# Another stored order, other PSUM banks and other eviction engines for a two-headed layer on one core

## The chip, the cores and the metric

The kernel runs on one core of a Trainium2 chip. The metric is the device time of one execution in microseconds. Three executions of the kernel before took 272.57, 272.51 and 273.82 us, a median of 272.57. The engines are named as the profile names them: PE (TensorE matmul), PEld (its weight load), DVE (VectorE), ACT (ScalarE), POOL (GpSimd) and SP (SyncE), whose queue issues nearly all DMAs.

## The reference

Two independent layers on 2048 tokens of width 640, concatenated along the features.

```python
# A: short filter, gate, long convolution by FFT, gate
k_shift = sum(k_pad[:, t:t+S] * shift_k[:, ks-1-t] for t in range(4))
kv = k_shift * v
y = irfft(rfft(kv, 2*S) * rfft(ssm_k, 2*S))[:S] + kv * ssm_D
a = q * y
# B: 32 heads of 20, four segments of 512 tokens, a memory carried from segment to segment
q, k, v = x @ wq, x @ wk, x @ wv
for s in range(4):
    p = softmax(q_s @ k_s.T * scale + causal_mask)
    a_mem = (phi(q_s) @ M) / (phi(q_s) @ z + 1e-6)     # phi(t) = t + 1 or exp(t)
    o = sigmoid(beta) * a_mem + (1 - sigmoid(beta)) * (p @ v_s)
    M, z = M + phi(k_s).T @ v_s, z + phi(k_s).sum()
b = o @ wo
out = concat(a, b)
```

## The kernel before

The program is recorded first and issued afterwards. `conv`, `project`, `attend` and `project_out` call proxies that store every operation (line 150, `Recorder.add`) with its dependencies; matmuls that belong together make one operation, and operations that share PSUM make a group. `issue` (line 247) then issues all 1543 operations in the order that the packed table ORDER gives, and binds each of the 486 PSUM groups to the bank that the packed table BASE gives. PSUM is one tile, `ps`, of eight banks of 128 x 512 f32. All instructions carry line 256, the line of the issuing call, so the rows are told apart by their tiles. The semaphore waits follow from the dependencies and the banks, so the order on each engine and the bank numbers decide who waits for whom: an engine takes its instructions in order, and an instruction that waits holds up all behind it.

Layer A (`conv`, line 428) goes over five slices `dp` of 128 features. The filter `ssm_k` is brought to `kT` with time on the partitions, by PE transposes for slice 0 and through a DRAM copy (`turned`) for the others. `k` arrives transposed in `kr`; the short filter is PE work against diagonal matrices `skd` (`ks` groups), and DVE multiplies by `vt`. `spectrum` (line 515) makes DFTs with the table `Wf`, whose results are evicted to `F` (`FK` for the filter, `FX` for the signal), with butterflies on DVE into `Kh` and `Xh`. `product` (line 548) is DVE alone (`pq`, `Y`), and `inverse` (line 584) is PE against `Wi` and a DVE multiplication by `q` in `pq`.

Layer B goes over eight units u: segment s = u // 2 and a half of the heads. `project` (line 636) computes K, Q and V from `xT` against `wqkv`, five matmuls of 320 columns for each 128 tokens, evicted to `KQ` and `Va`. K and Q are transposed to `KQT` (by PE for u = 0, by DMA otherwise), `phi` goes to `PP` and `PqT`. A bound on the scores is worked out from the largest |k| (`kmx`, transposed on PE, reduced by DVE into `kam`, then `A`, `qabs` and `bT`) and four small DMAs write it as a row of `KQT`. `attend` (line 722) makes scores on PE in row groups of 32, 384 or 256 columns wide below the diagonal, and with a mask from `pack` on the diagonal. ACT turns each two banks into `ET` by an exponential of 1024 columns, 160 of them in all. PE then sums values (`Va` with `ET`) and memory (`Mbd` with `PqT`), and DVE divides (`rr`, `o`, `o_s`). `project_out` (line 815) multiplies by `wo`; for the last segment PE transposes `o_s` into `xT` first, and the outputs are evicted to `PP` and `outb`.

An eviction copies a PSUM group to SBUF. `evict` (line 387) looks up which engine does it in the string EVICT (line 863), a digit for each of 238 evictions: "1" is DVE, "0" ACT.

```python
    def evict(self, out, in_, grp):
        e = self.evicts
        self.evicts += 1
        if EVICT[e] == "1":
            self.nc.vector.tensor_copy(out=out, in_=in_, grp=grp)
        else:
            self.nc.scalar.copy(out=out, in_=in_, grp=grp)
```

Twenty warm-up matmuls on a cleared tile `o` stand at the start of PE's order. They write nothing that is used.

Of the kernel before, what the change touches and what calls it, by code (L numbers as in the profile page):

```python
# [865 lines left out]
ORDER = r"""
c-jTQ1ArU=3<SVzHo3ZA+qP}nwr$&A+qP}nwr$(iOpwHu2ohIHNIZ!z2_&H;lEjikl1eg3E-56Xh@=uqYDpt$C7q;~@KRn>%1Q>wBjqH&l$LN(QZh;fsV!wBl0Zx{NlnQsrKGw<m3&fF>PTd9sU}6Gve
b}PQbjUL0VyOArLF{|zEqTY(o$kdEh#7sB%W51XwqDYNfgN{4JC!f*W%Jb3QH2rqbW6?7LiPvSMzITZ7hu>fo9QS+C-X4NJ*-xG=yZ;_R?00Yct6v9VL#mmeg88OKL7nsG+2Tl+t#RMRIE=DXm|%jbza
1l1!89S}CGsw7(S9vN}Kp${@+8ou#MrmU7xfx=MHHE4`$=c9T9*K?`XC%`VxrpY)K5nnTiPPARBqHCPJk3>_k?q_U3J2^vF&%4*4>Id!J4lflwhr)hRgr@3XARMolKM4M`Qt)z)`xFpu~vP4J7G94+?b
&V|5c{)l)OI@9>%e9`a(FIyxCu%KSCZT1FRMBd>Nw&x&t*v#mx;E3XvRXID9BrY|xLLMJE?K3Eb-Xm!jS`)+bhaLnaWYjK=vrMa6C{X@w4olB1CosEGy;=zpG=a2l8_UnhdNfuWZ5AtH4($edTphxwWs  # L870
cq_BvI1X?(7b4LU`(Ne7M1Hri1)>L%SSvn2s{%68c=d*q0;)lNE4kID+&D}!{V1nU-EshxGQZq|01f?Kt#PSI&HLuN^6Y|}2<U867@=SdCirYYG^r%P1!*JH9sE=UN(VE_yDgdCT}a#FS{5E9`zK(EOn
oi97Jw_cP}(pOK*ZjH+uGDkw8riQ^_9jWQqM{mg`Ny|MtSFXzr9i^i+1Jm=SMCLBNEJO5;+?CrhM$gDlP0C?<PBQX}oR`x&Tw}=s8LK1otc=rGyeelkEHd$gp3zf!Ptq_I!{MYZl>3sJS@=*6X*`C<5s
ie%2*P2#tM@blmdH>pm8^Uq_w}e=(TEtv$8t;+k7PQt@v08wa30sEvR|LbAok}Bj$n2k(1V(Tw=@@X@|uoeG+fuc`b^I0dA*}Ca9c0vMct=2^tnXGO^t=HlA8mV05Or7v5|)_<$*TB1ip}&Oo)1TsQEa
N1$apx=_JnLWJcsG$xGsyCT1c;;$@A&7y3q?>uX8Ew-U^l9LvObC-3F4KGl~R1+VmpzSgKH$kH6gH(H4A)$mn5=t6$f`7FbDD9g|CNvAMA;^2dPl)@as{2a;8`bDO4Fyo>zX7iK0)lvMSO;CdKSc*R+3
DV)6CdE&wk2y?^1<Zhw{3AvASCU~gGvWgmF+Ga$n`A;tq(K%eW^txPMShp2$cz@K%t}mwZ1^QhnH9~E3)7ebMYxICQI5Hh6Xp3^LfU5LK^0bIH7?^8R%a+{%?hl|Hmt$?sKdHk&be&MnyklW2yJ0(1>3
PcYq337vMn00HCk{y+hG+GS_iIX8?@pQwnR(j!y4vAD+F00Ys84Qmj9$N3!n+xBbGH~B#UjSkQyD3*a|`r!QxndM6-r$#^zkl!sv`1?1G-`#klrOd$S`uVgOQDAMQgZcIG-BL3B%ET^QLqp)dZb@VlnA
e)y+_(3MdPjA7lljoX>hx-*si(!TtmX)J*iL0a3vpBmM6au<JVJPT{_Z3C5uSQN=^H~(mQ>xv^BZ4EHV(%E5lgLASKM=|tcI2&kt7~V?Y0LEAb>y6M1a4-8{KT08^mBv1nM0XtJF>YkA9p?$2WLXTd9y
rCy7;Ir!2KzbI4sx6wU@z;5-j>xaGm~v)X6uEDxXLU>_OXyGhbydvn>6;dLx^c-c$N)O9_JW}r+J>)>;iA`Hj`QfWVee<X7~AkdF&b=av<{B6dQ#byu(~J)oNf6uJbMj;~+-ZBi>_8JmwQV<t65{U_9e
^8-ka7#o_jvIV`um;WP}zXpF#f&an`jXaj7d&9q4vhiZ7ik$B6)n2yQFXS3`b``IoOu-R4}?>QdRY&iPcbQ@+vte_3UTpNQzHo=Y}zs;~>_S)vzF$}f&HUU*I7A0&V3fmM^MR8kTMXadRLP?v7@>anXS
}CiIiZ%n4thAM}%C^WB+i6s>vbMw;+Zh~3Ih&2>-qh-%i8ZiB7Q?IB3DiM6pM_C&5;GCj8(Ms?Ys)MwtJz0Zw{Tw1>RSz)i``giH7%;2!g8x+(Y&@L_Gae3!UF!4aeNM1SQ~3=pV-{yA)>Fb`Jmr~`EA  # L880
@nBwv7b7TK?2rF~<2i|ZY%rQJbjPvW7xj;*q!ehq7_wRN<MSZ52-%EEYZzl2|0jNja1oox}i*fzV2PS({{TQ`f~TkSJ9T6as~J?sj;aI+=yA57r8>?b!_Z2!)lw%fXU4<F$PeUDv7OpoGA(9ZW@r2k<`
--~6qfmps2+bxwZ#||6hJFSDK_FzxrXR+5h`g)}G^Eik0zRxaT1y*9e9k7Fz&JWpPJ7Ryi8tMI_{o_%)WNXmZFWXuS@PSS{ZpZ9|owO^q3Yoo+ueW4wcFNqs`&Bz_{rrpt?5v5wuGu*Y^09sw7c8US$1
uN#O*n7YZ5<xqh7I?Z*o=p`X-{$29^szdw+#Lq&+q~d>@^<RIDdsV$nKA<t7r1}81Fg#mUZ(F_>3)>=sElg?$~X6Y+I4b-y)As@{f38Pw)xv@YHhqGkb22k;TV&Hh*CSyo*ovmzLEFc?kcCDIU@{;0LC
9LC@>ouo2s^9liZK@_R)u?D@QiSMpa@)Q5U8-vPDCKHaBzb+6&SP~2<!PR#HPR>FJwPgL<zKGS=7C$H+Ay`)$3(q6{PdI<Z2H&)JT`D`!m4Sbf*@!H<d8+l#-jS61J8+(6$YxVuJy|X4>&%fATEcXxA)
c@hVt@MvJ!58`ppX;JuZLlx)dA`W!`zM2bvjslNRhxNpZ{aPyl`nDX5FhP7Y^k?))1S7=+qmmrTjt;GpRM(_zRuVCY7gid-|b;_gNM^!w$V5F9uJ}7d;PZ^^v%A-L+MukWAMX%$hY}+-{E0&ryutle$u
1qP2cCCHKd;K{T@s2cyx`e2RxD<@m+q`Px)y->SsK%p7rp0(Qo-VKjxP_j-Ge*sCvOK`xU?KL3+<MaNqy>RgbIBJfeQ_Yku7y_(PANU;T&wa|V9;FaPZpkia+hz$1U}&;7AK@faFKU-)<b;4$@&Bk<7!
f!F@jU-~D1<FEX!zw^)jAN3y$Z2
"""
# [76 lines left out]
```

## Time and profile before

| | |
|---|---|
| median of three runs | 272.57 us |
| span of the profiled execution, first to last instruction | 272.0 us |
| PE busy | 260.8 us, 4368 matmuls |
| DVE busy | 250.9 us, 424 instructions |
| ACT busy | 248.8 us, 388 instructions, 160.6 us of it in the 160 exponentials |
| DMA | 43.74 MB, mean 161 GB/s |
| mean granted clock of TensorE | 0.993 |

The busy time of PE counts a matmul from its start to a modelled end, and matmuls overlap, so 96% does not mean that PE could take no more. In a timeline row the first number is the start, the second the time that the row covers, then come engine, line, operation, tiles and shapes, and in brackets the idle time of the engine before it, with what ended it. In a row of windows the busy time of each engine stands with its count of instructions, then the granted clock as a share of full speed, the DMA share and GB/s. The profiled execution has no separate time of its own in the table: its span is 0.57 us below the median.

### The profile page before, as it was taken

Reading aid. Unit: us, or ns where it says so; the run is one execution under the profiler, and the core shown is the slowest. Engines: PE = TensorE matmul, PEld = TensorE weight load, DVE = VectorE, ACT = ScalarE, POOL = GpSimd, SP = SyncE. Lnnn points to the kernel's source line nnn. Section 1 sums busy time; section 2 is a strip of 40 time slices with the busy share of each in tenths; the row PEclk is TensorE's granted clock in tenths of the full one; section 3 lists DMA queues with packets and bytes.
Section 4 is the critical chain, followed back from the end, with each engine's and each line's share of the span. In section 5 each row is a group of like instructions: output and inputs, shape, how many; then the busy total and the mean of one; then the engine's idle time right before and its main releaser. Section 6 shows DMA issues by size and latency. Waiting matters only on the chain.

```text
span 272.0 us, 10130 instructions
## 1 busy us (share of the span) xinstructions
PE 260.8 (96%) x4368; PEld 195.4 (72%) x4371; DVE 250.9 (92%) x424; ACT 248.8 (91%) x388; POOL 6.9 (3%) x18
## 2 busy tenths in 40 slices
...
PEclk9999999999999999999999999999999997999999
...
GB/s 166 347 207 243 82 191 225 311 194 172 170 217 201 144 195 195 191 178 159 159 165 190 116 151 226 147 197 65 146 177 82 4 154 27 169 155 90 27 68 133
DMA packets 126972, 43.74 MB, mean 161 GB/s; under 512 B 117339, under 2 KB 124512, under 8 KB 126800
## 3 DMA queue, kind: packets, MB, share of 16 engines
...
q8 instruction: 34, 0.56, 0.9%
q0 software_dynamic: 160, 0.20, 0.2%
...
## 4 chain that ended last, share of the span: by engine, by line
PE 55%; ACT 33%; issue 6%; DVE 4%; ACTq 0%; DVEq 0%
PE ps L256 55%; ACT ET L256 21%; ACT F L256 4%; ACT KQ L256 3%; ACT PP L256 3%; ACT outb L256 1%; ACT Va L256 1%; DVE F L256 1%; DVE pq L256 1%; DVE Kh L256 1%; ACT bT L256 1%; DVE qabs L256 0%; DVE vt L256 0%; DVE Xh L256 0%; DVE PP L256 0%
## 5 line engine op out<-in xcount | busy, mean ns | idle before, releaser
L256 ACT ACTIVATE ET<-ps 128x1024 bf16<-128x1024 f32 x160 | 160.6, 1102 | 1.9 <-PE ps L256 1.7
L256 PE MATMUL ps<-wqkv,xT 128*128 128x320 bf16 x480 | 76.3, 300 | 0.5 <-ACT ET L256 0.3
L256 PEld LDWEIGHTS <-xT 128*128 128x128 bf16 x640 | 58.1, 98 | 25.7 <-issue 5.2
L256 PE MATMUL ps<-Va,ET 128*128 128x21 bf16 x1280 | 42.4, 172 | 0.3 <-ACT ET L256 0.3
L256 ACT CAST F<-ps 128x512 bf16<-128x512 f32 x69 | 42.0, 687 | 0.3 <-PE ps L256 0.3
L256 PEld LDWEIGHTS <-ET 128*128 128x128 bf16 x1280 | 39.7, 96 | 3.0 <-issue 2.2
L256 PE MATMUL ps<-KQT 32*128 32x128 bf16 (+2 forms) x896 | 34.6, 240 | 1.1 <-ACT ET L256 1.0
L256 PEld LDWEIGHTS <-Wf 128*128 128x128 bf16 x320 | 28.9, 97 | 6.1 <-issue 1.5
L256 ACT CAST KQ<-ps 128x320 bf16<-128x320 f32 x61 | 28.2, 496 | 1.4 <-PE ps L256 1.3
L256 PE MATMUL ps<-wo,xT 128*128 128x320 bf16 x160 | 25.4, 299 | 0.0
L256 PEld LDWEIGHTS <-KQT 32*128 32x128 bf16 x896 | 16.0, 92 | 10.9 <-issue 9.9
L256 PE MATMUL ps<-vt,Wf 128*128 128x256 bf16 x160 | 22.4, 272 | 0.1
L256 PE MATMUL ps<-kT,Wf 128*128 128x256 bf16 x160 | 22.2, 273 | 0.2 <-ACT ET L256 0.2
L256 PE MATMUL ps<-Y,Wi 128*128 128x256 bf16 x160 | 21.7, 280 | 0.0
L256 DVE TENSOR_TENSOR o<-ps,rr 128x640 bf16<-128x640 f32 x24 | 19.5, 814 | 0.2
L256 PE MATMUL ps<-Mbd,PqT 128*128 128x84 bf16 x96 | 18.1, 202 | 1.2 <-ACT ET L256 0.9
L256 DVE TENSOR_TENSOR Y<-Y,pq 128x2048 bf16<-128x2048 bf16 (+1 forms) x20 | 18.6, 945 | 0.0
L256 DVE TENSOR_TENSOR pq<-Xh,Kh 128x2048 bf16<-128x2048 bf16 x15 | 18.1, 1209 | 0.0
L256 PEld LDWEIGHTS <-Wi 128*128 128x128 bf16 x160 | 15.3, 100 | 3.5 <-issue 1.0
L256 ACT ACTIVATE PP<-KQ 128x640 bf16<-128x640 bf16 (+1 forms) x18 | 17.7, 991 | 0.0
L256 PE MATMUL ps<-pack 32*128 32x128 bf16 x512 | 14.7, 216 | 1.9 <-ACT ET L256 1.7
L256 ACT CAST Va<-ps 128x320 bf16<-128x320 f32 x31 | 15.0, 520 | 1.2 <-PE ps L256 1.2
...
## 6 DMA issues: line engine op xcount, KB each, us to landing
...
```

What stands on the lines that cost most here:

```text
L256: f(*[fix(a) for a in args], **{k: fix(v) for k, v in kw.items()})
```

## The change

The program, its operations and their shapes stay. Three tables are replaced: EVICT, ORDER and BASE. In EVICT 36 of 238 digits differ, and DVE has 29 evictions instead of 31, ACT two more. ORDER is another order of the same 1543 operations, which differs on every engine and in SP's queue, and BASE gives other banks. The rows of the two packed tables say nothing to a reader and are cut to their first line.

```diff
-EVICT = ("10000010100101001001010000000000000000000000000000000100000000000000010100000000000000111000000000100000000000000000000000001000000000000000"
-         "00000000000000000001001110000000000000100000000001001010010000000000010000000001000000000110000101")
+EVICT = ("1101000001000110000100110000000000000000000000000000000000000000000000010000000000000011100000000000100001000000000000000000000000000000"
+         "000000000000000000100010000100000001000000010000001001010000010010000000010000000001010001000000000000")
 ORDER = r"""
-c-jTQ1ArU=3<SVzHo3ZA+qP}nwr$&A+qP}nwr$(iOpwHu2ohIHNIZ!z2_&H;lEjikl1eg3E-56Xh@=uqYDpt$C7q;~@KRn>%1Q>wBjqH&l$LN(QZh;fsV!wBl0Zx{NlnQsrKGw<m3&fF>PTd9sU}6Gve
...
+c-jrt(_$D35CqWK+1=E(ncB8(+qP}nO4`)6ZQHhO8~6Uhc{ov!011%@iID_xkrY5OltLWjLvjQn1yUjvQX>sYqdf8>BC;SW3LpkzqBu&RB#5*~hxCYmvdDmpD1!<pf{Mt5Y^a3n$bq8B422;oav~Q5<xm|pQ46&Z
...
 BASE = r"""
-c-mD{0TRO?2m=KC|Br_uST|2?tAvoS5RoNW!|TcG*+eC3oHwmElk>~^V))`X+nCC;UDJSLb*jKgL@M4F(9Vs<SL{6w-p0wfWta-o#YiQusNKmznMv_Q$k*|7#;ND9Qp7iYl3QQ~ZgdS+yJPJ*!Jgb3rz
...
+c-lo%3l_sL2-0Zu{x_Zi>DHIdzd~%ASy<YgQ|5Dy^;lM3kB#QzT~Ex@^WX3sc=nx$PuMqaW42z7yxPTaRStL$&c^T^k~g;$TT|~v_BU6I9+>u^+RkX`w^@{ZH0G}Dz|QIUE5xv-p(@ciX5E}Z)<uuj1b1Q&e1`so
...
```

Four places of the new order, in words. At the start, two tiles of x are loaded before the first part of the DFT table, and the transposes of `kT` and x stand between warm-up matmuls on PE. In the segment s = 3, half 0, a value projection and the `kmx` transposes stand before a group of masked scores that they followed. In the segment s = 1 the `kmx` transposes stand behind masked scores that they preceded. At the end, all eight last output evictions are on ACT.

More of the change, by code (lines that the diff above doesn't have):

```diff
@@ L865 @@
 KQW, FW, WW = 1, 1, 1
 ORDER = r"""
-c-jTQ1ArU=3<SVzHo3ZA+qP}nwr$&A+qP}nwr$(iOpwHu2ohIHNIZ!z2_&H;lEjikl1eg3E-56Xh@=uqYDpt$C7q;~@KRn>%1Q>wBjqH&l$LN(QZh;fsV!wBl0Zx{NlnQsrKGw<m3&fF>PTd9sU}6Gve
-b}PQbjUL0VyOArLF{|zEqTY(o$kdEh#7sB%W51XwqDYNfgN{4JC!f*W%Jb3QH2rqbW6?7LiPvSMzITZ7hu>fo9QS+C-X4NJ*-xG=yZ;_R?00Yct6v9VL#mmeg88OKL7nsG+2Tl+t#RMRIE=DXm|%jbza
-1l1!89S}CGsw7(S9vN}Kp${@+8ou#MrmU7xfx=MHHE4`$=c9T9*K?`XC%`VxrpY)K5nnTiPPARBqHCPJk3>_k?q_U3J2^vF&%4*4>Id!J4lflwhr)hRgr@3XARMolKM4M`Qt)z)`xFpu~vP4J7G94+?b
-&V|5c{)l)OI@9>%e9`a(FIyxCu%KSCZT1FRMBd>Nw&x&t*v#mx;E3XvRXID9BrY|xLLMJE?K3Eb-Xm!jS`)+bhaLnaWYjK=vrMa6C{X@w4olB1CosEGy;=zpG=a2l8_UnhdNfuWZ5AtH4($edTphxwWs
@@ L871 @@
[L871 to L886, printed above, removed]
@@ L887 @@
-f!F@jU-~D1<FEX!zw^)jAN3y$Z2
+c-jrt(_$D35CqWK+1=E(ncB8(+qP}nO4`)6ZQHhO8~6Uhc{ov!011%@iID_xkrY5OltLWjLvjQn1yUjvQX>sYqdf8>BC;SW3LpkzqBu&RB#5*~hxCYmvdDmpD1!<pf{Mt5Y^a3n$bq8B422;oav~Q5<xm|pQ46&Z
+4Q)^#1yL8p;HZNJh=)9=iW-Q7$f%5JXoz|UKqFK^Av8vG6h=$5LO$ka6J%jlreZTBWNPMO0VZNo6l6)3U@0bM5~g7>wnht-W=Eu8XOv-Creu2*XD4()2jpg3v_mY!MmB~<T4rK7W@mY3W^;5!H*`l23`8F0Wnc70
+AM{603`Q9ALj|ryC=9|7ROA3uVr3@hTxMV|EaOlN$2=C{a?WQUGcpHraskuvE2}a+gE$PqY|7@G$yuDjsSJyxY{p3}%E?^9rL4{>tj}a@$U<C&btudcXuvwG%Nop$dfbFj7>W4Ei`5*Bu^5L97=!UxjrEv-nry+A
@@ new lines @@
++=69j#Wf6JOr6b1*oZZlh&ha<TTzXhv6hq3i0jyxO&CeH;Q;nwJN9EL_Fz3%@E~?z3RZG2W^gfAu_HS%vWCM>q|k7ZQfFfqc4IjX;V^1(1ADO#d$TjAVI#M26F0Lp+c2JX;S988JGSRmZsTAMVOJ*6>FB^z+KoY&
+g`_%^sWliOn8uk%q|=#LyR#?b>k&lP+B}M5*vTGT$OO8Gix5KxFoL=a<UA}!L><Jw?8lQ>iQPPbG0dRHv4?XojAOY1r!ky!(Vtf^f+Kkf>GcwBVH7j!Ud~4*&8*`%o)dT#S@br}AV4PaGP3Cn+{6W3#5IiOS?pja
+xsKC3%QHNO^9Umgun^fbq29q=+`|c;WN3*f+j)qQ<P@XnVaC=t8ddHxtlY;DK14Kmfbg;eOA$dHA&uVWQQl)@8LY>+kH?uqqexuc#UUC+uP~~L1nOg4Wm?_OgKQ<&c%3=*0G}eACX_@nN=Iuhy}?_2g7|WWH~9=x
+HGxdi+)Bx#w|S1|d4U&siB04IpW`wga)c(+y!sN4m{pVONR2J|w1B?A1bv0L5>Li!9GR%k_?#+}HL<+p8%)ur@`|tdhHsff^6Lw}#y}mU!8%iu%3~&zcPy+=*-V~rmd2E~h$ZhCq6>A5eqdRhujTb4-=Um-;#hr;
@@ new lines @@
+&n%)JFk9znbcrFQw6vN`*BSbSW%Mh)p}3aNkNAv|`U%P93;tlJ4%5F#AwLi(KQT`$YZc8TnWd<vlkcdi3v`_R!dy)+)ii_rMoOu!i!_T&(u`6=vq}XmriFC4R?^h+L2GI*X(_d|qNb8Ol2;b%CatZTHAt6gHpwl^
+G>0^owi?>%Xm+WqTQsNSllEFr>uG&$pzSoQg|mj*LY8ZIgt122K|AUSZ7;2~pmfre+FCnETUn*6wSYvjHk!oNXgf)2-?>&JTN7=nQLMG(myVJ~zA>sb)8^Vz3rh=aBmdAz3Q00cZtFC@C9t>_)3)hf?$9L~%ZkcB
+Zr9G*MZ0P@{l(b!gYm4frm~;xrM<O}{wAcmc9$MfM0#jy>n{VOr>3#Kn%4U1PTi$3ES>e&Vv^pXS#;a239Y!Km6UcwGTM4Qq(>CGRZEDdYXb>yL+uX(bg&)Pk`lp&*&a<~LoAbxv%Nai_Q^i&Do6F0PP4=|-bzU~
+39Hm_T1NKk0X?oKw6vVmKpUW^bf9d|gPPeoOA0$6WhJx@k}eWPPwRfUtXDLPWwqX-+Q<4xc_}9m?W$(CzBa)&>P@XIre}1b-PW^uPS5KFZ78?2r}UD(a$oz&L(OJY<f7)VoR+~FNkzG&(`|-TkV?|e`rBZ6pw~2?
@@ new lines @@
+-O&72ORno39V(6Go{p7AT2&tF6Md?8b%>0UiBemh=>QuhFZGo^*WvO)U+WvqWs{_kz14R*%LZBvsVVO@$O>C-D`KOigiW$IHp+%uNgE^6WwecuQg%?rScr|6sWL%=ZH`U0K~_yh*eIE8)1;^sv$<AXf~1bjv&k|;
+f@OgnmAX>gN?UlHA{DKYm9ffJ#SY0rD{IGOrcAMNR^ARvRa<0>t(sM^(~{TnSW|0eOYF5BmopN}o7-$@WR0!5oscG$(3jdtnI*A3hR?J_eo8{*qmHy?Hc|>$D2?g$t%23BnpVqdTODg?bEK|?_Xxh+T39`qD=X})
+e$!pj%G~SAJXvWi?Yi8M03T}?WxlkwOVZW~+JgV-m|vA^64vKiJ!@lI?6dBct+r6wS$q4U9jv2uvbDC(!ud^EW$}EQMe$#{(QZj+i|Ud6w{Eidp1?O-7mMbfw5uiaMbgc>TXOGVJuQyM^~G{tF34rMBE9Uk+>xZd
+%l6n0{i!{@mxuAavfDcNSve<(J&A9(ofhazB&F}LWs=I5%U@0HOJ%in@-&{-S4d~?Z4v#u{?l~6M@D;e|D%z-qmS|QzSs8K5FhIMEQKGigLcRcTLxb#{rrga_lvg1GI~~5TPK<Qk{z`{e%X%OdRZl_<%F3H_LDZj
```

11 lines of the change are left out of this document (8 added, 3 removed).

## The prediction

> **What bounds the kernel now.** I read the page first, for its sums and its clock row.
>
> ```profile
> span 272.0 us, 10130 instructions
> PE 260.8 (96%) x4368; PEld 195.4 (72%) x4371; DVE 250.9 (92%) x424; ACT 248.8 (91%) x388; POOL 6.9 (3%) x18
> PEclk9999999999999999999999999999999997999999
> ```
>
> Three engines are nearly full, so no average tells which one matters. One slice in 40 shows a TensorE clock below full. The chain of waits, in order of time, comes next; its first and last long pieces are these (start, us, engine).
>
> ```profile
> 1.26 18.64 PE ps L256 x147
> 19.95 12.40 PE ps L256 x116
> 32.41 8.88 PE ps L256 x116
> ...
> 254.90 13.70 PE ps L256 x220
> 268.62 0.43 ACT PP L256
> ```
>
> The start belongs to PE without a hole, and so does the end. Between them the chain hops between ACT's ET (the exponentials) and PE. So I cut the span at the first and the last exponential on ACT, whose timeline rows are these, with every wait of ACT over 0.2 us that lies between them.
>
> ```profile
> 33.66 1.98 ACT L256 ACTIVATE ET<-ps 128x1024 bf16<-128x1024 f32 x2
> 116.47 0.43 ACT L256 CAST KQ<-ps 128x320 bf16<-128x320 f32 x1 [0.25 <-PE ps L256]
> 117.25 3.77 ACT L256 ACTIVATE ET<-ps 128x1024 bf16<-128x1024 f32 x4 [0.35 <-PE ps L256]
> 227.45 5.61 ACT L256 ACTIVATE ET<-ps 128x1024 bf16<-128x1024 f32 x6 [1.34 <-PE ps L256]
> 259.30 2.03 ACT L256 ACTIVATE ET<-ps 128x1024 bf16<-128x1024 f32 x2
> ```
>
> The table of windows for the three parts (length; then busy us of PE, PEld, DVE, ACT, POOL; granted clock; DMA):
>
> ```profile
> 0.00:33.66 33.66, 32.29 (x279) 23.88 (x282) 23.35 (x42) 20.20 (x42) 6.94 (x18) 1.00 0.85 210
> 33.66:261.33 227.67, 221.29 (x4002) 166.31 (x4002) 222.64 (x374) 225.47 (x341) 0.00 (x0) 0.99 0.83 156
> 261.33:272.00 10.67, 7.25 (x94) 5.26 (x90) 4.87 (x10) 3.11 (x7) 0.00 (x0) 0.99 0.35 103
> ```
>
> The middle is ACT's: busy 225.47 of 227.67 us, 2.20 idle, of which the three waits are 0.25 + 0.35 + 1.34 = 1.94. DVE idles 5.03 there. The whole is 33.66 + 227.67 + 10.67 = 272.00. The median of the runs, 272.57, is 0.57 above this span; I carry the 0.57 along. A difference under 0.5% (1.36 us: 271.21 to 273.93) cannot be told from none.
>
> **The change part by part.** No instruction is added or dropped except that 36 evictions change engine, so each term is a matter of when.
>
> *Work on ACT in the middle.* Counted from the digits of EVICT and the stored order, ACT has 95 casts of 320 columns and 68 of 512 between its first and last exponential before, 93 and 69 after. The price of one in a run of them comes from two rows.
>
> ```profile
> 25.14 2.68 ACT L256 CAST F<-ps 128x512 bf16<-128x512 f32 x5
> 36.29 1.48 ACT L256 CAST KQ<-ps 128x320 bf16<-128x320 f32 x4
> ```
>
> A cast alone takes 0.59 and 0.43 there, so the next ones cost (2.68 - 0.59)/4 = 0.52 and (1.48 - 0.43)/3 = 0.35. The term is -2 x 0.35 + 0.52 = **-0.18 us**. DVE, with 5.03 of slack, covers the one 320-column cast more (13 for 12) that it gets, against one 512-column cast fewer (5 for 6).
>
> *The stretch at half clock.* ACT's wait of 1.34 us has a cause. The table of windows in steps of 3.4 us, at the two emptiest windows for PE and the two after:
>
> ```profile
> 81.60:85.00 3.40, 2.59 (x40) 1.81 (x41) 3.40 (x6) 3.40 (x5) 0.00 (x0) 1.00 1.24 225
> 221.00:224.40 3.40, 2.33 (x61) 1.63 (x58) 3.37 (x7) 3.40 (x5) 0.00 (x0) 0.94 0.98 173
> 224.40:227.80 3.40, 3.40 (x27) 2.02 (x25) 2.76 (x4) 2.06 (x4) 0.00 (x0) 0.56 0.06 4
> 227.80:231.20 3.40, 2.76 (x66) 2.02 (x64) 2.77 (x6) 3.40 (x5) 0.00 (x0) 1.00 0.20 49
> ```
>
> PE is busy 2.33 us in the emptiest one, and right after it the granted clock is 0.56; with 2.59 it stays 1.00. The hole itself, on PE's timeline:
>
> ```profile
> 221.32 0.40 PE L256 MATMUL ps<-KQT 32*128 32x384 bf16 x8
> 222.10 0.23 PE L256 MATMUL ps<-pack 32*128 32x128 bf16 x2 [0.39 <-ACT ET L256]
> 223.02 0.40 PE L256 MATMUL ps<-pack 32*128 32x128 bf16 x14 [0.69 <-ACT ET L256]
> ```
>
> PE sits 0.39 + 0.69 = 1.08 us because the next scores (`pack` is the mask) need PSUM banks that ACT's exponentials still hold. PE before, from that place:
>
> ```order
> L256 MATMUL ps<-KQT_86 128x384
> ...
> L256 LDWEIGHTS pack
> L256 MATMUL ps<-pack 128x4x32
> L256 LDWEIGHTS KQT_86
> L256 MATMUL ps<-KQT_86 128x128
> ...
> L256 LDWEIGHTS xT_100
> L256 MATMUL ps<-wqkv,xT_100 128x320
> ...
> L256 LDWEIGHTS kmx
> L256 MATMUL ps<-ident,kmx 128x128
> ```
>
> and PE in the changed kernel, from the same `KQT` scores:
>
> ```order
> L256 MATMUL ps<-KQT_86 128x384
> ...
> L256 LDWEIGHTS kmx
> L256 MATMUL ps<-ident,kmx 128x128
> ...
> L256 LDWEIGHTS xT_100
> L256 MATMUL ps<-wqkv,xT_100 128x320
> ...
> L256 LDWEIGHTS pack
> L256 MATMUL ps<-pack 128x4x32
> ```
>
> The kmx transposes and a value projection now stand ahead of the blocked scores. Their price, from rows that stand alike 105 us earlier:
>
> ```profile
> 115.59 0.84 PE L256 MATMUL ps<-wqkv,xT 128*128 128x320 bf16 x5
> 116.27 0.39 PE L256 MATMUL ps<-ident,kmx 128*128 128x128 bf16 x4
> 116.59 0.40 PE L256 MATMUL ps<-pack 32*128 32x128 bf16 x16
> ```
>
> From start to start that is 116.27 - 115.59 = 0.68 and 0.32, together 1.00 of the 1.08 us. The window would hold about 3.3 us of work instead of 2.33, above the 2.59 that kept the clock. The bounds for this term are 0 (the clock falls all the same) and -1.34 (ACT's wait goes whole); I take **-1.34**, since 3.3 is on the far side of 2.59.
>
> [...]
>
> *The waits at 116.* ACT's 0.35 us ends with the masked scores that begin at 116.59. Before, four kmx transposes stand ahead of them on PE; in the changed order they stand behind. The places, before and after:
>
> ```order
> L256 LDWEIGHTS kmx
> L256 MATMUL ps<-ident,kmx 128x128
> ...
> L256 LDWEIGHTS pack
> L256 MATMUL ps<-pack 128x4x32
> L256 LDWEIGHTS KQT_86
> L256 MATMUL ps<-KQT_86 128x128
> ```
>
> ```order
> L256 LDWEIGHTS pack
> L256 MATMUL ps<-pack 128x4x32
> L256 LDWEIGHTS KQT_86
> L256 MATMUL ps<-KQT_86 128x128
> ...
> L256 LDWEIGHTS kmx
> L256 MATMUL ps<-ident,kmx 128x128
> ```
>
> The scores come 0.32 us sooner: **-0.32**, between 0 and -0.35. What is late next is the max over kmx on DVE, by the time of 16 + 16 score matmuls, inside DVE's slack.
>
> *The start.* SP's queue is reordered, before and after:
>
> ```order
> L256 DMA kT_102<-in_A_ssm_k_dram 128x2048
> L256 DMA ident<-c_ident 128x128
> L256 DMA Wf<-c_wf 128x1024 x2
> L256 DMA Y_101<-in_B_x_dram 128x640 x2
> L256 DMA Wf<-c_wf 128x1024 x2
> ```
>
> ```order
> L256 DMA ident<-c_ident 128x128
> L256 DMA kT_102<-in_A_ssm_k_dram 128x2048
> L256 DMA Y_101<-in_B_x_dram 128x640 x2
> L256 DMA Wf<-c_wf 128x1024
> L256 DMA Y_101<-in_B_x_dram 128x640
> ```
>
> Two tiles of x (`Y`) overtake the DFT table `Wf`. On PE, 13 warm-up matmuls instead of 18 stand ahead of the first `kT` transposes; the x tiles follow; the other 7 warm-ups fill in behind. PE's work ahead of the first scores is the same set, and PE has no hole there, so only a new hole could move the first exponential. The rows for it (SP's issue of x, PE's warm-up and first use of x, and what had been moved by 3.7 and 5.7 us, GB/s last):
>
> ```profile
> 2.60 0.91 SPq L256 DMA_DIRECT2D Y<-in_B_x_dram  x2
> ...
> 1.26 6.16 PE L256 MATMUL ps<-o 128*128 128x512 bf16 x18 [1.26 <-DVE o L256]
> 10.23 0.44 PE L256 MATMUL ps<-ident,Y 128*128 128x128 bf16 x5
> ...
> 0.00:3.70 3.70, 2.44 (x6) 0.88 (x7) 0.33 (x1) 1.28 (x1) 3.14 (x10) 1.00 0.47 158
> 0.00:5.70 5.70, 4.44 (x11) 1.61 (x12) 0.33 (x1) 1.28 (x1) 5.14 (x15) 1.00 0.62 171
> ```
>
> 18 warm-ups take 6.16 us, so 13 end near 1.26 + 13 x 0.34 = 5.7. By then 5.7 x 171 = 975 KB have been moved, and what is queued up to the second x tile is 885 KB (32 + 512 + 2 x 160 KiB). That puts PE's wait at nearly 0. The other bound: x was used 10.23 - 2.60 = 7.6 us after its issue; issued as fourth (about 2.1) it is there by 9.7 at worst, and PE, at it by 6.4 (eight transposes and five more behind 5.7), would stand 3.3 us. I take **0**, by the bytes.
>
> *The end.* All eight last output casts and the last two transposes' casts go to ACT (three output casts and one of 512 columns were DVE's).
>
> ```profile
> 264.61 3.98 PE L256 MATMUL ps<-wo,xT 128*128 128x320 bf16 x28
> ```
>
> PE gives 28 matmuls in 3.98, so a group of five every 0.71 us in the last two groups, and ACT needs 0.35 to 0.43 per cast; the cast that ends the chain is one of ACT's as before, behind the same last group. **0**, bounds +0.35 (one cast of backlog) and 0.
>
> The sum: 272.00 - 0.18 - 1.34 - 0.32 = 270.16, and with 0.57 it is **270.7 us**.
>
> **The rivals.**
>
> *The clock falls all the same (26%).* What fills one hole is missing elsewhere. A second value projection also comes forward, from 233.58 to the place after the score matmuls near 229; its row, and the window that it leaves:
>
> ```profile
> 233.58 0.84 PE L256 MATMUL ps<-wqkv,xT 128*128 128x320 bf16 x5
> ...
> 231.20:234.60 3.40, 3.21 (x64) 2.10 (x64) 3.40 (x7) 3.40 (x7) 0.00 (x0) 1.00 1.15 242
> ```
>
> 3.21 - 0.68 is 2.53, between the 2.33 that lost the clock and the 2.59 that kept it. Against: later work slides in. Price: the 1.34 stays, 272.57 - 0.18 - 0.32 = 272.1; no change that can be measured.
>
> [...]
>
> *The start starves (22%; slower).* PE takes its queue in order: if the second x tile, or `kT`, lands after 6.4 us, everything behind it waits, the other warm-ups too, and ACT, whose order now has an x cast ahead of its first `kT` cast. Each us moves the first exponential by as much, and a hole over the 1.08 us of above takes the clock down as well, at 1.34. So from a hole of 1.1 us on the kernel is slower than before (270.7 + 1.1 + 1.34 = 273.1), from 1.9 us on by over 0.5%, and at the bound it is 270.7 + 3.3 + 1.34 = 275.3. For it: that bound, and that nothing else can fill the hole. Against: the bytes.
>
> *The second filter waits (5%).* SP now sends the transposed load of the next `kr` behind three small row copies that wait for ACT, and one load; before it went ahead.
>
> ```profile
> 23.88 2.45 SPq L256 DMA_TRANSPOSE kr<-in_A_k_dram  x1
> 29.21 0.69 SPq L256 DMA_DIRECT2D KQT<-bT  x1
> 32.41 0.82 PE L256 MATMUL ps<-skd,kr 128*128 128x384 bf16 x6
> ```
>
> It was used 32.41 - 23.88 = 8.5 us after its issue. Issued near 29.21 + 4 x 0.69 = 32.0, it is there between 34.4 (its own 2.45) and 40.5; PE has ten more groups ahead of it now, eight of 0.68 and two of scores, and comes near 32.41 + 8 x 0.68 + 2 x 0.3 = 38.5. The wait is 0 to 2.0, at worst 272.7: no change that can be measured.
>
> **How the numbers follow.** The forecast has 47%. Its own range goes down to 269.5, by one more wait of ACT ahead of the first exponential, whose row follows, and the other one at 116 (0.93 + 0.25), and up to 271.7 (half of the clock term and the 116 term lost).
>
> ```profile
> 30.81 0.43 ACT L256 CAST Va<-ps 128x320 bf16<-128x320 f32 x1 [0.93 <-PE ps L256]
> ```
>
> Of the 47, 41 are faster and 6 the same. The falling clock: 1 faster, 23 same, 2 slower (two more such stretches). The starved start: 3 same, 19 slower. The second filter: 5 same. That is faster 42%, same 37%, slower 21%. The range from 269.5 to 274.4 leaves out what of the forecast lies below it and the starts with a hole over 2.4 us, less than 2 in 10.
>
> **What would show it.** Right: a clock row of 9s up to the end; ACT's idle time between its exponentials near 0.4 us; the first exponential within 0.5 us of 33.66; the last within 10.7 us of the end. Wrong: PE idle ahead of the first x transposes, or a first exponential past 35; another digit under 9 in the clock row, with an ACT wait over 1 us behind it; ACT waits of more than 2.2 us in all in the middle, whatever ends them.

## The result, and the profile after

The changed kernel takes 274.53 us, the median of 18 runs (273.27 to 276.06); the kernel before, run beside it, takes 272.69 (18 runs, 272.29 to 273.82). The ratio is 1.0056, with a 95% interval of 1.0043 to 1.007: slower by about 0.6%. The forecast of 270.7 and its upper end, 274.4, both lie below.

The page of the changed kernel, its span and its clock row:

```profile
span 272.2 us, 10146 instructions
PEclk9999999999999999999999999999999999999999
```

The clock row is full, as forecast, and the execution took 273.95 us, 1.75 more than its span. That offset is 1.7 to 1.8 in every execution whose span is known, and before's first profile (span 272.0) must then be the slowest of its three runs, 273.82, and not the median. A second profile of before, without the half-clock stretch of the first one at 224 us, has a span of 271.3 and a time of 273.08. Here are the tables of windows, cut at the first and the last exponential (length; busy us of PE, PEld, DVE, ACT, POOL; clock; DMA), of the changed kernel and then of that second profile:

```profile
0.00:35.38 35.38, 33.15 (x280) 24.02 (x283) 24.45 (x44) 20.41 (x40) 6.79 (x18) 1.00 0.75 191
35.38:261.08 225.70, 219.50 (x3995) 165.84 (x3995) 222.74 (x374) 225.23 (x341) 0.00 (x0) 1.00 0.83 157
261.08:272.20 11.12, 7.48 (x96) 5.54 (x94) 2.94 (x6) 4.48 (x11) 0.00 (x0) 1.00 0.44 134
```

```profile
0.00:34.47 34.47, 33.21 (x281) 24.06 (x282) 23.34 (x42) 20.19 (x42) 6.92 (x18) 1.00 0.81 205
34.47:260.66 226.19, 219.87 (x4003) 165.66 (x4002) 222.47 (x374) 225.32 (x341) 0.00 (x0) 1.00 0.85 157
260.66:271.30 10.64, 7.25 (x94) 5.26 (x90) 4.86 (x10) 3.10 (x7) 0.00 (x0) 0.94 0.35 104
```

Start +0.91, middle -0.49, end +0.48. The middle did what was forecast: ACT is idle 0.47 us in it instead of 0.87 (2.20 in the first profile). The loss stands at the two ends. About half of the 0.48 at the end lies behind ACT's last cast and belongs to this execution: 3.1 us follow that cast here and 2.9 in before, but also 2.9 in e9, a second profile of the changed kernel. PE's timeline at the start, after:

```profile
1.26 5.51 PE L256 MATMUL ps<-o 128*128 128x512 bf16 x13 [1.26 <-DVE o L256]
11.15 0.62 PE L256 MATMUL ps<-ident,skd 5*64 5x5 bf16 x12 [0.73 <-DMA skd<-in_A_shift_k_dram]
11.70 2.90 PE L256 MATMUL ps<-kT,Wf 128*128 128x256 bf16 x25
34.93 0.40 PE L256 MATMUL ps<-KQT 32*128 32x384 bf16 x8
```

and in the second profile of before:

```profile
4.64 3.58 PE L256 MATMUL ps<-o 128*128 128x512 bf16 x10
9.48 0.60 PE L256 MATMUL ps<-kT,Wf 128*128 128x256 bf16 x4
10.01 0.62 PE L256 MATMUL ps<-ident,skd 5*64 5x5 bf16 x12
33.99 0.40 PE L256 MATMUL ps<-KQT 32*128 32x384 bf16 x8
```

Twelve tiny matmuls (the `taps` of the short filter, from a 5 KB load called `skd`) wait for their load, and the DFT of the filter (`kT`, `Wf`) stands behind them. On POOL's queue, after:

```profile
1.21 0.70 POOL L256 DMA_DIRECT2D pack<-c_pack  x1 [0.76 <-POOLq L948]
4.04 0.51 POOL L256 DMA_DIRECT2D skd<-in_A_shift_k_dram  x1
```

and the start of the chain of waits, after, which in before was PE alone from 1.26 us on:

```profile
4.04 7.06 DMA skd<-in_A_shift_k_dram
11.15 10.92 PE ps L256 x105
```

Before, POOL issued `skd` at 2.45 us, and it landed within 3.9 to 5.7 us in the profiles with that order. The trace also records the packets of a load: the first of the five of `skd` (1 KB each, some 0.05 us) begins at 9.04 us after, 5.0 us behind the issue, and at 4.92 before, 2.5 behind it, while the last one of `pack` is done at 5.4 after. So 5.0 of the 7.1 us go by ahead of the first packet, and the five themselves take 0.23.

The raw times of the first scores mislead, since the first row of warm-ups takes 5.60 to 6.96 us with 18 of them and 4.36 to 5.73 with 13, in the profiles of the table below. The first clock record of a trace is one of the full clock, at 5.54 us in before's first profile and at 7.18 in the second; in the first, a warm-up takes 634 ns ahead of it and 379 behind it, and one follows the other every 0.43 and 0.22 us. (The clock column prints 1.00 where no record stands.) What repeats is the time from the end of the first row of warm-ups (18 before, 13 after) to the first scores. Five more warm-ups stand inside it after; a row of three takes 0.81 and a row of one 0.38, so 0.215 each, and 1.08 is taken off.

| kernel (run) | warm-ups end | first scores | between, like for like | wait on skd |
|---|---|---|---|---|
| before, two profiles | 7.42, 8.22 | 33.17, 33.99 | 25.75, 25.77 | 0, 0 |
| other runs with before's start (e7, e8, e12 to e15) | 6.86 to 7.92 | 32.63 to 33.68 | 25.75 to 25.77 | 0 |
| before, POOL's order of after (e5) | 7.52 | 34.36 | 26.84 | 1.01 |
| after, two profiles (e9 the second) | 6.77, 6.99 | 34.93, 35.45 | 27.08, 27.38 | 0.73, 0.90 |
| after, POOL's order of before (e2, e11) | 5.96, 5.97 | 33.56, 33.85 | 26.52, 26.80 | 0, 0 |
| after, taps moved back (e10) | 5.62 | 35.01 | 28.31 | 0 |

So the new start costs 1.3 to 1.6 us in these two profiles, and 0.8 to 1.0 of it stays without the wait on `skd`. In e2 and e11 PE stands idle for 0.17 and 0.62 us of that; what makes the rest is not resolved. From the first tap matmul to the first scores it is 24.0 us in every profile with PE's old start and 23.8 in every one with its new start (e10, which moves the taps, left aside), whether the taps waited or not. So the loss stands ahead of the taps. Where PE waits on `skd` in the changed kernel, the taps begin with the landing (it lands at 11.1 and 11.65 us, they begin at 11.15 and 11.65), so quicker warm-ups would only have made that wait longer.

### The profile page after: what moved, and what is told of

It reads as the page before. It is cut to its first block, busy times and chain, and to the rows that moved or that the text cites. A ratio compares the mean times of both kernels' runs of the same rounds, so it can differ in the third digit from the quotient of the medians.

```text
span 272.2 us, 10146 instructions
## 1 busy us (share of the span) xinstructions
PE 260.1 (96%) x4368; PEld 195.4 (72%) x4371; DVE 250.1 (92%) x422; ACT 250.1 (92%) x390; POOL 6.8 (2%) x18
## 4 chain that ended last, share of the span: by engine, by line
PE 51%; ACT 23%; DVE 12%; issue 6%; DMA 5%; POOL 1%; SPq 1%; DVEq 0%; ACTq 0%; POOLq 0%
PE ps L256 51%; ACT ET L256 14%; DMA skd<-in_A_shift_k_dram 3%; ACT F L256 2%; ACT PP L256 2%; DMA pq<-in_A_q_dram 2%; DVE pq L256 2%; DVE Xh L256 2%; ACT KQ L256 1%; DVE Y L256 1%; DVE vt L256 1%; ACT outb L256 1%; DVE Kh L256 1%; DVE F L256 1%; ACT bT L256 1%
## 5 line engine op out<-in xcount | busy, mean ns | idle before, releaser
L256 ACT ACTIVATE ET<-ps 128x1024 bf16<-128x1024 f32 x160 | 163.9, 1135 | 0.3 <-PE ps L256 0.2
L256 ACT CAST F<-ps 128x512 bf16<-128x512 f32 x70 | 43.2, 694 | 3.2 <-PE ps L256 3.1
L256 PE MATMUL ps<-Va,ET 128*128 128x21 bf16 x1280 | 41.8, 172 | 0.0
L256 PEld LDWEIGHTS <-ET 128*128 128x128 bf16 x1280 | 39.1, 96 | 2.3 <-issue 0.9
L256 ACT CAST KQ<-ps 128x320 bf16<-128x320 f32 x55 | 26.5, 514 | 1.8 <-PE ps L256 1.5
L256 PE MATMUL ps<-vt,Wf 128*128 128x256 bf16 x160 | 21.3, 272 | 0.1
L256 PE MATMUL ps<-Y,Wi 128*128 128x256 bf16 x160 | 20.6, 273 | 0.3 <-ACT ET L256 0.3
L256 ACT ACTIVATE PP<-KQ 128x640 bf16<-128x640 bf16 (+1 forms) x18 | 18.5, 1037 | 0.0
L256 PE MATMUL ps<-skd,kr 128*128 128x128 bf16 (+4 forms) x114 | 16.0, 254 | 0.8 <-ACT F L256 0.6
L256 PEld LDWEIGHTS <-kr 128*128 128x128 bf16 x116 | 14.5, 149 | 2.1 <-issue 0.8
```

The source lines that it names most:

```text
L256: f(*[fix(a) for a in args], **{k: fix(v) for k, v in kw.items()})
```

## The experiments

Two theories at first. A: the loss stands at the start, in PE's in-order queue, and at the end, and the middle is a little better; the half-clock stretch belongs to some executions only. B: the loss comes from the middle, or the hole at 222 us makes the stretch each time. "At full clock" are below those executions whose mean granted clock is 0.998 or more; the others, at 0.986 to 0.994, hold at least one half-clock stretch and are called executions with a dip.

**e1, the kernel before again.** No edit.

> The kernel before, unchanged, to see span and clock of each execution. Theory A (the dip of the clock is an accident of some executions, and the profiled one of before had it): time minus span is 1.7 to 1.8 us in every execution; those with a clock of 0.999 or 1.000 have a span near 270.8 and a time near 272.5, those with 0.993 or 0.994 a span near 272.0 and a time near 273.7. Theory B (the hole at 222 us makes the dip each time, as the prediction had it): every execution shows 0.993 or 0.994, and the time is about 0.6 above the span.

272.96 us (12 runs; ratio 0.999, 0.9977 to 1.0002). Time minus span is 1.7 to 1.8 throughout, and 3 of the 12 executions have a dip. Over all runs of it whose clock is on record, before has one in 68 of 122 executions, with medians of 272.7 to 272.8 at full clock and 273.3 to 273.7 with the dip. Theory A holds for the dip: executions that have it are 0.5 to 0.9 longer, and they are a good half.

**e2, after with GpSimd's order of before.**

```diff
 (POOL)
-DMA pack, zero kb, zero kr, DMA bt, zero KQ x2, DMA skd, zero Mbd, zero Drow, DMA Drow, ...
+zero Drow, zero Mbd, DMA Drow, DMA bt, DMA skd, zero KQ, DMA pack, zero kr, ...
```

> The changed kernel with GpSimd's 14 instructions in the order of before, so that skd (shift_k) is issued at about 2.5 instead of 4.04 us. Theory A (PE's queue stands behind the tap matmuls until skd lands): no wait on skd, the first exponential 0.7 us sooner, at 34.6, and a median near 273.8. If taps are not what the start waits for (the x tiles, or ACT's order of casts): first exponential at 35.2 to 35.5, median unchanged near 274.5. If pack, now issued 3 us later, is needed early: a first exponential past 35.4 and over 274.5.

272.90 us (11 runs), ratio to before 0.9986 (0.9977 to 0.9995): from 1.0056, the loss is undone (at full clock 272.90 against 272.83) by the order of 14 instructions of an engine that is busy 3% of the span. No execution has a dip. PE's rows:

```profile
1.26 4.70 PE L256 MATMUL ps<-o 128*128 128x512 bf16 x13 [1.26 <-DVE o L256]
9.78 0.62 PE L256 MATMUL ps<-ident,skd 5*64 5x5 bf16 x12
33.56 0.40 PE L256 MATMUL ps<-KQT 32*128 32x384 bf16 x8
```

No wait on `skd`. The gain of 1.2 to 1.6 us is more than the 0.73 expected. The landing fits that, though it is not shown: both profiles that waited had slow warm-ups (5.51 and 5.73 us for the 13, 4.70 here), and behind 4.36, as in e10, the landing of the first one would mean a wait some 1.1 us longer.

**e3 and e4, start of one with the rest of the other**, cut at the first exponential.

```diff
-ORDER, BASE, EVICT of one kernel
+e3: before up to the first exponential, after from there; e4: the reverse
```

> All operations up to the first exponential in the order, on the engines and in the banks of before, the rest as in the changed kernel (five groups moved to other banks where the two meet). Theory A (the start costs the 1.7 us, the middle is no worse): first exponential near 33.7, and 33.7 + 225.7 + 11.1 + 1.75 = 272.2 us. Theory B (the loss comes from the middle or the end, and the late start is made up by slack): 274 or more.

> The other way round: the changed kernel's operations up to the first exponential, then the order, engines and banks of before (one group moved). Theory A: first exponential near 35.4, middle 226.3 and end 10.7 as in an execution of before without the dip, 35.4 + 226.3 + 10.7 + 1.75 = 274.1 us. Theory B: the time of before, 272.5 to 272.7.

277.76 us (ratio 1.0154, 1.0125 to 1.0182) and 277.48 (1.0149, 1.0136 to 1.0162). Neither fits: e4 misses both theories, and e3 lies in theory B's open range but 3 us over the changed kernel itself. At that place one order has done operations that the other has not, and ACT waits up to 1.61 us behind the seam, at 36 to 52 us. They decide nothing; e13 cuts at a better place.

**e5, before with GpSimd's order of after**, the edit of e2 the other way round.

> The kernel before with GpSimd's instructions alone in the changed order (skd issued at about 4.04 us behind the load of pack). Theory A (PE's queue stands behind the tap matmuls until skd lands near 11.15 us; in the repeat of before they began at 10.01, in its first profile at 9.19): PE waits 1.1 to 2.0 us on skd, the first exponential comes at 35.6, and the median is 1.2 to 1.9 us over that of before, 274.2 to 274.9. Theory C (GpSimd's order matters only together with the new order of PE): as before, within 0.3.

275.37 us (6 runs), ratio 1.0081 (1.0049 to 1.0113). PE waits 1.01 us on `skd`, and the first scores come 1.08 later, like for like:

```profile
10.38 0.62 PE L256 MATMUL ps<-ident,skd 5*64 5x5 bf16 x12 [1.01 <-DMA skd<-in_A_shift_k_dram]
```

POOL's order alone makes the start late, without the new order of PE. Five of six executions have a dip, two of them at 0.986, so the median lies above the 274.2 to 274.9 expected; the one at full clock has 273.65, 0.9 over those of before. With the start later by 1.08 us five of six executions have a dip, where before has one in 68 of 122; these runs do not give a reason.

**e6, after with pack behind skd.**

```diff
 (POOL)
-DMA pack, zero kb, zero kr, DMA bt, zero KQ x2, DMA skd, zero Mbd, zero Drow, DMA Drow
+zero kb, zero kr, DMA bt, zero KQ x2, zero Mbd, zero Drow, DMA skd, DMA pack, DMA Drow
```

> The changed kernel with one load of GpSimd moved: pack (184 KB) is issued behind skd instead of ahead of it; two small memsets moved ahead keep the issue of skd near 3.9 us. If skd's 7.1 us from issue to landing come from pack standing ahead of it in the same queue: it lands 4.4 to 4.9 us after its issue, near 8.6, no wait on skd, median near 272.9 like the run with all of GpSimd's order. If they come from the bulk loads on the other queue: it lands near 11.0 as before this edit, and the median stays at 274.2 to 274.5.

273.55 us (12 runs), ratio 1.0014 (0.9998 to 1.003), between the two expectations. `skd`, issued at 4.16, took 6.6 us and landed at 10.8, with 0.53 us of wait, so the 184 KB of `pack` ahead of it are not the main reason why it is slow, as the packets say too; the median is 0.5 to 1.0 lower all the same. With an issue at 4.0 to 4.2 it took 6.3 to 7.7 us in six profiles, with one at 2.45 it took 3.9 to 5.7 in eleven. What slows it by 2 us is left open.

**e7, e12 and e15: the prediction's two moves in the middle, together and each alone**, in the kernel before.

```diff
 (e12 and e7, PE near 116 us)
-kmx transposes, masked scores
+masked scores, kmx transposes
 (e15 and e7, PE near 222 us)
-masked scores, value projection, kmx transposes
+kmx transposes, value projection, masked scores
 (e15 and e7, ACT)
-exponential, cast of the value projection, exponential
+cast of the value projection, exponential, exponential
```

> The kernel before with two moves alone: at 222 us the kmx transposes and the value projection ahead of the blocked masked scores (as in the change), at 116 us the masked scores ahead of the kmx transposes. If both terms of the prediction hold: no execution with a clock of 0.992 to 0.994 (about half of before's have it, at 0.9 us each), no wait of 0.35 on ACT at 118, and a median near 272.3 against 273.0 to 273.2. If the dip of the clock does not hang on this hole: executions with 0.993 in the same share, and a gain of 0.3 only.

> The kernel before with one swap on PE: at 116 us the masked scores ahead of the four kmx transposes. The prediction's term: ACT's wait of 0.35 gone, 0.32 us off, median 0.2 to 0.3 under before. The rival from the run with both moves (waits of 0.42 and 0.28 us on ACT 2 and 5 us later, since the convolution matmuls then wait for DVE's max over kmx): 0.0 to 0.4 over before.

> The kernel before with the kmx transposes and the value projection ahead of the blocked masked scores at 222 us, nothing else. The prediction's term: no execution with a clock near 0.993, and a median at that of the full-clock executions of before, 272.7. The rival from the run with both moves (the transposes wait 1.18 us for DVE there, so the hole stays): executions with 0.993 as often as in before (half), and a median of 273.0 to 273.6.

Together 274.12 us (ratio 1.0033, 1.0014 to 1.0051), with a dip in 6 of 12 and 273.34 at full clock, 0.6 over before. The swap at 116 alone: 274.0 (1.0023, 0.9999 to 1.0048); its executions at full clock have 272.44, 0.39 under those of before, as the term of 0.32 said, but 6 of 12 have a dip, at 274.9. In its profile, one with a dip, the wait of 0.35 is gone and two others have come, on ACT:

```profile
119.89 1.94 ACT L256 ACTIVATE ET<-ps 128x1024 bf16<-128x1024 f32 x2 [0.42 <-PE ps L256]
122.92 1.94 ACT L256 ACTIVATE ET<-ps 128x1024 bf16<-128x1024 f32 x2 [0.28 <-PE ps L256]
```

The move at 222 alone: 273.35 (0.9996, 0.9984 to 1.0009), with a dip in 5 of 12; its seven executions at full clock have 273.23, 0.5 over those of before. PE's timeline and the windows of that run:

```profile
222.79 0.38 PE L256 MATMUL ps<-ident,kmx 128*128 128x128 bf16 x4 [1.18 <-DVE o L256]
```

```profile
220.40:223.80 3.40, 2.22 (x55) 1.63 (x54) 3.40 (x6) 3.38 (x5) 0.00 (x0) 1.00 0.93 175
227.20:230.60 3.40, 2.53 (x63) 1.84 (x63) 3.40 (x9) 3.40 (x5) 0.00 (x0) 1.00 0.46 121
230.60:234.00 3.40, 3.40 (x46) 2.00 (x45) 3.40 (x4) 3.13 (x5) 0.00 (x0) 0.50 1.13 175
```

The transposes that were to fill the hole wait 1.18 us for DVE, so the hole is as large as before, and the move alone wins nothing. The window with 2.22 us of PE work kept its clock here, and the next thin one, 2.53 us, lost it.

**e8, start and end of before, middle of after**: the first 250 and the last 102 operations from before.

```diff
-ORDER, BASE, EVICT of after
+operations 1 to 250 and the last 102 as in before, the rest as in after
```

> The first 250 operations and the last 102 in the order, engines and banks of before, all between as in the changed kernel; cut where the two orders have done the same operations but for three or four. Theory A (the middle of the changed kernel is 0.5 us shorter, start and end of before are better): first exponential as in before (33.7 or 34.5 with the slower warm-up), middle 225.7, end 10.65, so 0.5 us under a like execution of before and no dip: median 272.0 to 272.5, ratio 0.996 to 0.998. If the middle is not better in itself: 272.9 to 273.2.

272.35 us (12 runs, 271.95 to 273.91), ratio 0.9977 (0.9962 to 0.9992): faster than both kernels. One execution of 12 has a dip, and at full clock it has 272.33 against 272.71.

**e9, the changed kernel again.** No edit.

> The changed kernel once more, for a second profile. Theory A (the taps are held until skd lands, whatever came before): PE's wait on skd ends at the landing, at 10.3 to 11.2 us; if the 13 warm-ups take less than the 5.51 us of the first profile, the wait is longer than 0.73 by the difference, and the first exponential stays at 34.6 to 35.4. If the start depends on the warm-ups alone, the wait stays 0.73 and the first exponential moves with them. Executions with a clock near 0.994 lie 0.9 us above the others, in a share of a third; a profile of one shows where.

274.08 us (12 runs), ratio 1.0042 (1.0026 to 1.0057). `skd` took 7.6 us this time, landed at 11.65, and PE waited 0.90; the first exponential came at 35.89. The wait ends at the landing, as A says, but the landing itself moved by half a us between the two profiles, from 11.1 to 11.65. Over both sets, 9 of 30 executions have a dip.

**e10, after with the taps behind the DFT.**

```diff
 (PE)
-taps x12, kT with Wf (eight groups), x transposes
+kT with Wf (eight groups), taps x12, x transposes
 (DVE)
-cast of taps, build of skd, cast of xT, casts of F x3
+cast of xT, casts of F x3, cast of taps, build of skd
```

> The changed kernel with GpSimd's late order kept, but the 12 tap matmuls moved behind the eight groups of kT times Wf on PE (and their cast and the build of skd behind those casts on DVE). Theory A (what costs is that everything queues behind them): no wait on skd, the first exponential as in the run with GpSimd's old order (34.0 with 13 warm-ups in 4.70 us, 0.8 later with 5.51), median 272.8 to 273.3. If the late skd also holds the convolution that uses it: PE waits ahead of the skd x kr matmuls, and 273.5 or more.

274.63 us (6 runs), ratio 1.0063 (1.0044 to 1.0082). A miss for A: the wait on `skd` is gone and nothing is won. In its profile the warm-ups were quick, and PE's rows with waits are:

```profile
1.26 4.36 PE L256 MATMUL ps<-o 128*128 128x512 bf16 x13 [1.26 <-DVE o L256]
6.83 0.17 PE L256 MATMUL ps<-bt,ident 1*128 1x32 bf16 x1 [0.44 <-DMA bt<-in_B_beta_dram]
7.46 0.45 PE L256 MATMUL ps<-ident,Y 128*128 128x128 bf16 x5 [0.47 <-DMA Y<-in_B_x_dram]
10.95 2.89 PE L256 MATMUL ps<-kT,Wf 128*128 128x256 bf16 x25 [0.41 <-ACT kT L256]
```

PE stands 1.32 us on `bt` (POOL's queue too), on the second tile of x, and on ACT, which casts `kT` late because an x cast and `em` stand ahead of it. Ahead of the `skd` with `kr` matmuls it does not wait, as the other expectation would have it. `skd` is only the last of several inputs for which the new start comes too early.

**e11, e2 with the end of before as well.**

```diff
 (on top of e2)
+the last 102 operations as in before
```

> The changed kernel with GpSimd's order of before and the last 102 operations in the order, engines and banks of before. Theory A (the end costs 0.46 by itself): end 10.65 instead of 11.2 after the last exponential, median 272.4 to 272.6 where GpSimd's order alone gave 272.9; the middle 225.6, no dip. If the end's loss is only shifted: 272.8 to 273.0.

272.95 us (12 runs), ratio 0.9997 (0.9983 to 1.0011), at full clock 272.88: no better than e2. In the profile the end is 10.6 long, as expected, but PE waits 0.20 on x and 0.18 on ACT at the start. The old end shows no gain here.

**e13, the first 250 operations of before, the rest of after.**

```diff
-ORDER, BASE, EVICT of after
+operations 1 to 250 (all engines) as in before
```

> The first 250 operations (all engines, GpSimd too) in the order, engines and banks of before, all the rest as in the changed kernel. If the start alone made the loss (1.3 us by the two profiles, brought to the same warm-up): a median 1.3 us under the changed kernel, 272.7 to 272.9, first scores 25.3 us behind the warm-ups as in every run with the old start. If the end costs its 0.46 as well: 0.4 over the run with start and end of before (272.35), so the same 272.7 to 272.9; if the end costs nothing: 272.3 to 272.5.

272.52 us (12 runs), ratio 0.9985 (0.9963 to 1.0006). PE's rows:

```profile
1.26 5.92 PE L256 MATMUL ps<-o 128*128 128x512 bf16 x18 [1.26 <-DVE o L256]
8.96 0.62 PE L256 MATMUL ps<-ident,skd 5*64 5x5 bf16 x12
32.94 0.40 PE L256 MATMUL ps<-KQT 32*128 32x384 bf16 x8
```

At this seam nothing is lost, and the start alone takes the changed kernel from 274.1 or 274.5 to 272.5. One execution of 12 has a dip. The profile is of the slowest of the 12, at 274.43; at 126 and 137 us it holds two waits on DMAs that no other profile has there, and the longer one is ACT's:

```profile
137.73 0.42 ACT L256 CAST outb<-ps 128x320 bf16<-128x320 f32 x1 [1.50 <-DMA out_dram<-outb]
```

So it stands for the start, not for the median.

**e14, the changed end alone in before.**

```diff
-ORDER, BASE, EVICT of before
+the last 101 operations as in after
```

> The kernel before with the last 101 operations in the order, engines and banks of the changed kernel. If the end costs 0.46 by itself: 11.1 us from the last exponential to the end instead of 10.65, executions at full clock with a median near 273.2 (272.7 to 272.8 before), ratio near 1.0017. If the eight output casts on ACT are what costs: the same time, with a gap between PE's last matmul and ACT's last cast that grows over 0.46 us. If it is only shifted from the middle: 0 within 0.15.

273.72 us (12 runs), ratio 1.0017 (0.9999 to 1.0036); at full clock 273.12 against 272.75, 0.37 more. PE's last matmuls and ACT's last casts:

```profile
264.57 3.97 PE L256 MATMUL ps<-wo,xT 128*128 128x320 bf16 x28
```

```profile
259.11 1.94 ACT L256 ACTIVATE ET<-ps 128x1024 bf16<-128x1024 f32 x2 [0.23 <-PE ps L256]
266.81 2.19 ACT L256 CAST PP<-ps 128x320 bf16<-128x320 f32 x6
```

ACT's last cast ends 0.46 us behind PE's last matmul (269.00 - 268.54), and it is 0.46 in the second profile of before as well (268.37 - 267.91): eight casts on ACT cost nothing. But PE begins the last 28 matmuls 3.52 us after the last exponential (264.57 - 261.05), where in before it is 3.28 (263.94 - 260.66).

## Why the prediction was wrong, point by point

**The base failed, by 1.2 us.** "The median of the runs, 272.57, is 0.57 above this span; I carry the 0.57 along." The offset is 1.75, and the profiled execution was one of those with a dip. The terms, summed against that span and carried with 1.75, would have given 270.16 + 1.75 = 271.9. Against the median, the term of 1.34 was in part a gain over an execution that the median did not stand for. The stretch comes and goes: 68 of before's 122 executions have one, and its second profile stayed at full clock through the same two holes of 0.39 and 0.69 us. The start differs from execution to execution too: the same 18 warm-ups took 5.60 us in the profile of e8 and 6.66 in that of e12.

```profile
1.26 5.60 PE L256 MATMUL ps<-o 128*128 128x512 bf16 x18 [1.26 <-DVE o L256]
```

```profile
1.26 6.66 PE L256 MATMUL ps<-o 128*128 128x512 bf16 x18 [1.26 <-DVE o L256]
```

**The start failed: taken as 0, measured as 1.3 to 1.6.** This is the step that turned a gain into a loss. "I take 0, by the bytes." The bytes were those of SP's queue. POOL's queue, which the change reorders too, was not looked at, and the 5 KB on it held PE for 0.73 and 0.90 us in the two profiles; of the rest, other inputs of the new start held it for 0.38 us in e11 and 1.32 in e10, and a part is not resolved. "PE's work ahead of the first scores is the same set" was wrong too: five more projection matmuls and four more transposes of K and Q stand ahead of them after, and seven fewer of `skd` with `kr`. From start to start that is 0.68 + 0.22 - 0.99 us, about nothing, which was luck. e13 gives the price of the whole start, 1.6 to 2.0 us on the medians and some 1.5 at full clock. e5 and e2 show that POOL's order is enough to lose 2.1 us on the median in the old kernel (1.08 of it in the start; five of the six executions have a dip) and to win 1.2 to 1.6 in the new one. The rival "the start starves", at 22%, was the right case, and its span of 273.1 to 275.3 holds the result. Its sign, a first exponential past 35, is there. Its holder was not the one named: `skd` was, and x only when the warm-ups were quick. That the span fits is in part luck: it was reckoned from a base 1.2 too low, with 1.34 for a clock that stayed full in both profiles of the changed kernel.

**The clock term failed in its mechanism.** "The kmx transposes and a value projection now stand ahead of the blocked scores." They do, but the transposes need DVE's maximum, and DVE's queue was not followed. PE's rows with waits in the first profile after:

```profile
223.31 0.40 PE L256 MATMUL ps<-ident,kmx 128*128 128x128 bf16 x4 [0.65 <-DVE kmx L256]
231.18 0.84 PE L256 MATMUL ps<-wqkv,xT 128*128 128x320 bf16 x5 [0.44 <-ACT ET L256]
232.29 0.41 PE L256 MATMUL ps<-pack 32*128 32x128 bf16 x16 [0.27 <-DVE o L256]
235.67 0.20 PE L256 MATMUL ps<-Mbd,PqT 128*128 128x84 bf16 x1 [0.55 <-ACT ET L256]
```

The hole of 1.08 became one of 0.65, and new ones stand at 231 to 236, where the second projection had been taken away, as the rival "the clock falls all the same" had said. The windows of e10, which has the changed middle, show the clock going there:

```profile
230.60:234.00 3.40, 2.59 (x71) 1.85 (x64) 3.40 (x6) 3.40 (x6) 0.00 (x0) 1.00 1.20 192
234.00:237.40 3.40, 2.85 (x97) 2.55 (x92) 3.37 (x6) 3.40 (x5) 0.00 (x0) 0.82 0.54 111
237.40:240.80 3.40, 3.40 (x45) 1.98 (x38) 2.75 (x6) 2.85 (x6) 0.00 (x0) 0.68 0.17 33
```

The first profile after had the same thin windows and the same waits, and kept its clock. The step "3.3 is on the far side of 2.59" made a threshold out of two windows of one execution. The clock records of three traces lie on a grid instead: the stretch at half clock lasts 3.41 us and begins a whole number of 3.41 us behind the first record of the full clock, 64 in before's first profile (5.54 to 223.99), 66 in e15 (5.30 to 230.58), 68 in e10 (4.08 to 236.19). Counted from that record, the second of the two holes ends 217.48 us later in before's first profile (5.54 to 223.02) and 216.68 in its second (7.18 to 223.86), so the same hole falls on another place of the grid. Whether that decides the fall is not shown, and PE's busy time in a window does not decide it alone: from 220.4 to 223.8 PE is busy 2.33 us in before's first profile, where the clock fell behind that window (0.53 in the next), and 2.38 in its second, 2.23 in e7 and 2.22 in e15, where the next window has 1.00. What the change did move is the share: 9 of 30 executions after and 68 of 122 before, but 4 of 59 in e2, e6, e8, e11 and e13, which have the changed middle behind a quicker start, 2 of 24 of them in e8 and e13 with the old one. Which part of the middle lowers it is open, since the move at 222 alone does not (5 of 12).

**The other terms.** ACT's work in the middle: forecast -0.18, measured -0.09 (225.23 against 225.32). The wait at 116: gone in the changed kernel, as forecast, and worth 0.39 at full clock in e12; by itself it brings other waits, which the new order around it avoids. The end: "0, bounds +0.35 and 0" was right for what it costed, the backlog of casts, and missed that PE's last groups begin 0.24 us later. e14 has +0.37 for the whole end at full clock; e8 and e13, which differ in it alone, have 272.33 and 272.52, +0.19; e2 and e11, which do too, show no difference (272.90 and 272.88). The second filter: no wait on its load shows in either profile after.

With the true base the sum is 271.9, and with 1.3 to 1.6 for the start and 0 to 0.4 for the end it is 273.2 to 273.9. From e8, which has the changed middle alone and 272.33 at full clock, the same two terms lead to 273.6 to 274.3. The executions of the changed kernel at full clock have medians of 274.2 and 273.9.
